# The second weight block decoded behind head 0's last exponential, and the decay sums written through GpSimd's queue: an attention and gated feed-forward kernel

## The chip, the cores and the metric

The program runs on one core of one Trainium2 chip. The time is device microseconds of one execution. The engines are TensorE (PE; its weight loads are PEld), VectorE (DVE), ScalarE (ACT), GpSimd (POOL) and SyncE (SP). SP does nothing but issue transfers; ACT and POOL issue some too, and such an instruction stands in the engine's own order like any other.

## The reference

```python
# q, k, v: (8, 8, 576, 64) f32; s: (8, 8, 576) f32; w_gate, w_val: (512, 1536); w_out: (1536, 512)
scores = scale * np.matmul(q, k.transpose(0, 1, 3, 2))
s_pos = np.maximum(s, 0.0)
cum = np.cumsum(s_pos, axis=-1)
bias = -(cum[:, :, :, None] - cum[:, :, None, :])
scores = np.where(causal, -1000000000.0, scores + np.minimum(bias, 0.0))
scores = scores - np.max(scores, axis=-1, keepdims=True)
attn = np.exp(scores)
attn = attn / (np.sum(attn, axis=-1, keepdims=True) + 1e-09)
x = np.matmul(attn, v)            # heads side by side: (4608, 512)
gate = 1.0 / (1.0 + np.exp(-(x @ w_gate)))
return (gate * (x @ w_val) @ w_out)
```

The three weights arrive as 64-bit floats (8 bytes for each number), so the kernel reads them as pairs of 32-bit words and builds 32-bit floats from them itself.

## The kernel before

**Attention.** 64 heads (8 batches of 8) are taken one after the other. A head has five query tiles, t = 4 down to 0, of 128 rows (the last of 64) against 576, 448, 320, 192 and 64 keys. A loop over ticks n emits one tile in each: scores on TensorE (`n_s`, L631, with a matmul that adds the mask, L518), one tick later the masked maximum on VectorE (`n_max`, L643) and the exponential on ScalarE (L644), then transposes of the exponentials (`n_turn`, L653, copied by ScalarE, L654) and the product with v (`n_av`, L662). Heads 0 to 7 are in f32; for these q and k are transposed on TensorE (`n_prep`, L614) and moved by ScalarE (L618, L619, L621). Later heads use f16 high and low parts and DMA transposes.

**Decay sums.** `cum` and `rel` hold the sums of all 64 heads, one head in a partition. `rel` is written to `cum_d` in DRAM (L167). Head 0's row is spread to 128 partitions by GpSimd from `rel` (L451); the row of each later head is read back from `cum_d` into `cr` (L447, SP's queue) and then spread (L451). `cr` has two buffers. `rel` shares the buffers tagged `rl` with the first loads of v for its squares (L184, GpSimd's queue).

**Weights.** Twelve blocks of w_gate and w_val (f = 0 to 11, 128 columns of each, 512 KB each in two transfers) and six of w_out are decoded in steps n. `weight_step` first issues the loads for which room comes free (`load_weight`; L284 on SP for blocks 0 and 1, L286 and L279 on ScalarE's queue for the rest), except in step 0, and then decodes its own block: a scaled copy on ScalarE (L298), three bit operations on VectorE (L299, L300, L301), eight small matmuls for the columns' bound (L310), their maximum (L313), the power of two of the scale (L332, L334), and the split into f16 high (ScalarE, L337) and low part (VectorE, L338). Raw words lie in `ws` for f divisible by 3, and else in parts of `w2all`, which is free until w_out's blocks are split into it; `t2f` and `io` are also used as room. Step 1 issues the loads of blocks 2 and 3.

**Feed-forward.** From tick 44 on, groups of 256 tokens by 128 hidden columns are put between the heads: 48 matmuls into `gv` (L714), tanh (L719), products (L721, L729, L730) and the output product (L745).

**Order.** A scheduler sets the order on each engine from the order of the code, priorities (`first()` raises that of heads 0 to 7) and its own simulated times; `tc.issue_after(ins)` makes it place what is inside behind `ins`. What runs on the chip is that fixed order on each engine, with semaphores between the engines. Before, steps 0 and 1 are both emitted at tick 0.

## Time and profile before

| | |
|---|---|
| runs | 1146.3, 1140.69, 1143.78 us; median 1143.78 |
| profiled execution | 1143.07 us |
| its span, first to last instruction | 1141.3 us |
| busy: PE, DVE, ACT, POOL | 1091.1, 829.2, 753.0, 201.2 us |
| granted TensorE clock, mean | 0.99 |

The page counts busy time of each engine over the span, and it names lines of the kernel (L298 is line 298). A group or row "out<-in" gives the buffers without their numbers; "[1.69 <-PE nt_ps L653]" behind a row is the idle time before it and what ended that. A row "SPq" or "ACTq" is an engine's issue of a transfer. In the table of stretches, PEclk is the granted clock and "DMA share" the mean busy share of the 16 DMA engines.

### The profile page before, as it was taken

To read this page: it belongs to the slowest core of one execution; us is meant where nothing else is said; L and a number is where in the kernel's file an instruction comes from. 1 tells how busy PE (TensorE), PEld (TensorE's weight loads), DVE (VectorE), ACT (ScalarE), POOL (GpSimd) and SP (SyncE) were. 2 spreads that over 40 slices of the span, in tenths; PEclk is the share of its full clock that TensorE was granted. 3 is DMA by queue.
4 is the path that set the end of the run, shared out by engine and by line. 5 is a ranking of instruction groups with operands and counts; after the bars stand their busy time and mean duration, and the time that the engine had idled before them with its cause. 6 is when DMAs were issued, how large, how long until landed. Compare 5 with 4: busy or idle time off the path is not lost.

```text
span 1141.3 us, 30312 instructions
## 1 busy us (share of the span) xinstructions
PE 1091.1 (96%) x11796; PEld 854.8 (75%) x11796; DVE 829.2 (73%) x2357; ACT 753.0 (66%) x1474; POOL 201.2 (18%) x471
## 2 busy tenths in 40 slices
PE   6897878899999999999999999999999999999998
PEld 4776766757787787788777777778877887787775
DVE  6758989876787777766565577777777779682854
ACT  5868667767786777676656577768776666343533
POOL 3302101022232222221111112212121212000000
PEclk9999889999999999999999999999999999999999
DMA  9776896997989798775736469787977664200000
GB/s 270 215 206 140 180 165 144 183 186 163 174 176 173 158 177 162 155 152 116 169 66 149 103 152 164 150 166 156 179 134 164 145 117 93 41 20 2 20 1 37
DMA packets 445357, 157.62 MB, mean 138 GB/s; under 512 B 403551, under 2 KB 435295, under 8 KB 445214
## 3 DMA queue, kind: packets, MB, share of 16 engines
q1 hardware_dynamic: 418974, 128.17, 57.6%
q10 hardware_dynamic: 23040, 16.78, 5.0%
q0 software_dynamic: 3200, 10.75, 2.6%
q8 instruction: 92, 1.51, 0.5%
q14 instruction: 51, 0.42, 0.1%
HBM read 56.92 MB, written 9.58 MB: 58 GB/s over the span
## 4 chain that ended last, share of the span: by engine, by line
PE 70%; DMA 9%; DVE 8%; issue 5%; ACT 4%; SPq 2%; POOL 1%; ACTq 0%; POOLq 0%; DVEq 0%
PE gv L714 33%; PE o L745 21%; PE tv L831 3%; PE s L491 3%; PE s L489 2%; DMA v<-in_v_dram 2%; PE ta L831 1%; DVE e L529 1%; PE av L564 1%; PE av L562 1%; PE av L563 1%; PE na_ps L662 1%; DMA T<-qk 1%; DMA w2all<-in_moe_w_out_dram 1%; DMA x<-x 1%
## 5 line engine op out<-in xcount | busy, mean ns | idle before, releaser
L714 PE MATMUL gv<-x,w 128*128 128x256 f16 (+3 forms) x6336 | 553.9, 245 | 9.8 <-DVE t2f L721 8.8
L714 PEld LDWEIGHTS <-w 128*128 128x128 f16 x6336 | 480.2, 98 | 63.4 <-issue 12.0
L745 PE MATMUL o<-w2all,h 128*128 128x512 f16 x1296 | 313.9, 379 | 1.9 <-ACT h L729 1.9
L530 ACT ACTIVATE e<-e,em 128x576 f32<-128x576 f32 x280 | 153.1, 556 | 88.8 <-DVE em L529 86.0
L745 PEld LDWEIGHTS <-h 128*128 128x128 f16 x1296 | 123.4, 98 | 109.1 <-ACT h L729 2.3
L511 POOL TENSOR_SCALAR_AFFINE_SELECT rl<-rl 128x128 f32<-128x128 f32 (+1 forms) x240 | 88.4, 369 | 499.2 <-DVE em L529 456.2
L529 DVE CUSTOM_DVE_ANT_0 e<-s,rl,qkcf 128x576 f32<-128x576 f32 x280 | 151.2, 544 | 28.8 <-PE s L491 12.8
L729 ACT ACTIVATE h<-t,hsc 128x256 f16<-128x256 f32 x192 | 96.3, 503 | 92.7 <-DVE t L721 90.4
L719 ACT ACTIVATE th<-gv,scb 128x256 f32<-128x256 f32 (+3 forms) x264 | 99.0, 403 | 65.5 <-PE gv L714 53.9
L539 DVE SCALAR_TENSOR_TENSOR p<-e,p 128x384 f16<-128x384 f32 x224 | 103.2, 499 | 41.1 <-ACT p L534 40.3
L721 DVE SCALAR_TENSOR_TENSOR t<-th,gv 128x256 f32<-128x256 f32 x168 | 69.7, 415 | 63.9 <-ACT th L719 63.8
L534 ACT ACTIVATE p<-e 128x1152 f16<-128x1152 f32 x112 | 111.9, 1000 | 3.4 <-DMA pt<-p 0.9
L730 DVE SCALAR_TENSOR_TENSOR h<-t,hsc,h 128x256 f16<-128x256 f32 x192 | 93.4, 487 | 27.4 <-ACT h L729 25.0
L562 PE MATMUL av<-v,pt 128*128 128x65 f16 x560 | 67.7, 193 | 2.5 <-DMA pt<-p 2.5
L451 POOL PARTITION_BROADCAST cr<-cr x63 | 59.4, 949 | 55.9 <-ACT th L719 21.1
L489 PE MATMUL s<-T 128*128 128x288 f16 (+2 forms) x246 | 64.5, 280 | 3.8 <-DVE em L529 3.0
L563 PE MATMUL av<-v,pt 128*128 128x64 f16 x560 | 67.7, 192 | 0.0
L564 PE MATMUL av<-v,pt 128*128 128x65 f16 x560 | 67.6, 194 | 0.0
L491 PE MATMUL s<-T 128*128 128x288 f16 (+2 forms) x246 | 61.5, 277 | 4.0 <-DMA T<-T 4.0
L562 PEld LDWEIGHTS <-pt 128*128 128x128 f16 x560 | 52.5, 98 | 8.3 <-DMA pt<-p 3.4
L563 PEld LDWEIGHTS <-pt 128*128 128x128 f16 x560 | 52.5, 97 | 4.5
L564 PEld LDWEIGHTS <-pt 128*128 128x128 f16 x560 | 52.7, 97 | 0.2
(209 smaller groups left out, 1539.9 us busy)
## 6 DMA issues: line engine op xcount, KB each, us to landing
v<-v SPq DMA_DIRECT2D x56, 162.5 KB
v<-in_v_dram SPq DMA_DIRECT2D x64, 128.0 KB
out_dram<-io POOLq DMA_DIRECT2D x32, 256.0 KB, 3.4
T<-T SPq DMA_DIRECT2D x82, 72.0 KB
t2f<-in_v_dram SPq DMA_DIRECT2D x20, 288.0 KB
qk<-in_q_dram SPq DMA_DIRECT2D x17, 288.0 KB
qk<-in_k_dram SPq DMA_DIRECT2D x17, 288.0 KB
w2all<-in_moe_w_gate_dram ACTq DMA_DIRECT2D x7, 512.0 KB
```

What stands on the lines that cost most here:

```text
L491: nc.tensor.matmul(ps[:, : b_ - a], lhs, T[i][:, 2, a:b_], start=False, stop=not mask)
L529: nc.vector.tensor_tensor_reduce(e, ps, r, c, MASKED, ALU.add, ALU.min, acc)
L530: nc.scalar.activation(e_t[t][:, :w], e_t[t][:, :w], AF.Exp, bias=acc, scale=-1.0)
L534: nc.scalar.activation(p_s[h_][:, 0], e_s[h_], AF.Copy, scale=PSCALE)
L539: nc.vector.scalar_tensor_tensor(flat[:, LOW[t] * P : (LOW[t] + t) * P], e_t[t][:, : t * P], PSCALE, flat[:, kb * P : (kb + t) * P], ALU.m ...
L562: nc.tensor.matmul(AV[i][:, t], hi, v_[:, D : 2 * D + 1], start=kb == 0, stop=False)
L563: nc.tensor.matmul(AV[i][:, t, 0:D], hi, v_[:, 0:D], start=False, stop=False)
L564: nc.tensor.matmul(AV[i][:, t], lo, v_[:, D : 2 * D + 1], start=False, stop=False)
L714: nc.tensor.matmul(ps[:, gv, a:e], w1[f][:, cc, gv, wl], x_of(b, cc)[:, xl, c0 + a : c0 + e], start=(c == 0), stop=(c == 3 * NC - 1))
L719: nc.scalar.activation(th[:, a:e], ps[:, 0, a:e], AF.Tanh, scale=scb[b][:, f : f + 1])
L729: nc.scalar.activation(h[:, 0], t2, AF.Copy, scale=hsc[:, f : f + 1])
L745: mm = nc.tensor.matmul(ps[:m], h[:, hl, tt * P : tt * P + m], w2[f][:, wl], start=(f == 0 and c == 0), stop=(f == NF - 1 and c == 2))
```

## The change

The write of `rel` to DRAM goes from SP's queue to GpSimd's. Step 1 is emitted at tick 5 instead of tick 0, and everything in it (its decode and the loads of blocks 2 and 3) is placed behind the exponential of head 0's tile 0, which is head 0's last. Steps 2 to 5 keep their ticks.

```diff
-    nc.sync.dma_start(cum_d, rel)
+    nc.gpsimd.dma_start(cum_d, rel)
...
-    qT, kT, nA = {}, {}, {}
+    qT, kT, nA, e_last = {}, {}, {}, []
...
-        nc.scalar.activation(e_t[t][:m, :w], e_t[t][:m, :w], AF.Exp, bias=acc, scale=-1.0)
+        ins = nc.scalar.activation(e_t[t][:m, :w], e_t[t][:m, :w], AF.Exp, bias=acc, scale=-1.0)
+        if (i, t) == (0, 0):
+            e_last.append(ins)
...
-            while n < NE and wnext["step"] < min(2 + n // 8, 6):
-                weight_step()
+            while n < NE and wnext["step"] < min((1 if n < NTL else 2) + n // 8, 6):
+                with tc.issue_after(e_last[0].ins) if wnext["step"] == 1 else ExitStack():
+                    weight_step()
```

Lines behind L644 carry numbers that are two or three higher in the changed kernel.

ScalarE at the start, from block 0's decode to head 0's last exponential. `e_80` holds tiles 4 and 3, `e_79` tiles 2, 1 and 0; "w2all<-w2all" is the decode of block 1. Before:

```order
L298 ACTIVATE wa_147<-ws_146 128x1024
L644 ACTIVATE e_80<-e_80,em_4_248 128x576
L298 ACTIVATE w2all<-w2all 128x1024
L644 ACTIVATE e_80<-e_80,em_3_274 128x448
L654 COPY p_1_82<-nt_ps_4_6_269 128x384
L186 ACTIVATE vsq_0_263,vss_262<-vsq_0_263 128x576
L286 DMA ws_146<-in_moe_w_gate_dram 128x4x256
L644 ACTIVATE e_79<-e_79,em_2_292 128x320
```

And now, from the same decode on:

```order
L644 ACTIVATE e_80<-e_80,em_3_249 128x448
L656 COPY p_1_82<-nt_ps_4_6_244 128x384
L656 COPY p_1_82<-nt_ps_3_3_257 128x384
L644 ACTIVATE e_79<-e_79,em_2_267 128x320
L656 COPY p_1_82<-nt_ps_3_0_262 128x384
L644 ACTIVATE e_79<-e_79,em_1_281 128x192
L644 ACTIVATE e_79<-e_79,em_0_301 64x64
L286 DMA w2all<-in_moe_w_gate_dram 128x4x256
L337 ACTIVATE w_0_66<-wa_147,wscale 128x8x128
L286 DMA w2all<-in_moe_w_val_dram 128x4x256
L186 ACTIVATE vsq_0_238,vss_237<-vsq_0_238 128x576
L286 DMA ws_146<-in_moe_w_gate_dram 128x4x256
```

Head 0's second exponential now follows its first, block 1's decode stands after the last row shown, behind head 0's fifth exponential, and the load of block 2 (into `w2all`) is ahead of that of block 3 (into `ws`). Block 2's decode stands behind head 1's second exponential.

SP's queue at the start, as a difference; `ws` and `w2all` are the loads of blocks 0 and 1, `v_0_159` is pair 0's v:

```order
 L284 DMA ws_146<-in_moe_w_val_dram 128x4x256
 L284 DMA w2all<-in_moe_w_gate_dram 128x4x256
-L167 DMA cum_d<-rel 64x576
 L284 DMA w2all<-in_moe_w_val_dram 128x4x256
 L463 DMA v_0_159<-in_v_dram 128x4x64 x2
 L464 DMA v_0_159<-in_v_dram 64x2x64
```

On GpSimd the issue stands directly ahead of the spreading of head 0's row (L451).

ScalarE later, where w_out's blocks are loaded and decoded, from the issue of a load into `t2f` (L279 and L286, just ahead of the first row) over a load into `w2all` to that block's decode ("wa_147<-w2all"). Before:

```order
L337 ACTIVATE w2all<-io,wscale 128x1024
L502 ACTIVATE rl_2784<-cr_2678,qkcf_2664 128x576
L502 ACTIVATE rl_2915<-cr_2795,qkcf_2664 128x576
L279 DMA w2all<-in_moe_w_out_dram 128x8x128
L286 DMA w2all<-in_moe_w_out_dram 128x8x128
L719 ACTIVATE th_9_1765<-gv_9_1740,scb_1272 128x256
L337 ACTIVATE w2all<-wa_147,wscale 128x1024
L428 ACTIVATE qk_13_2803<-qk_6_2262,qksc_2662 96x6x64
L430 ACTIVATE qk_13_2803<-qk_6_2262,qksc_2662 96x6x64
L298 ACTIVATE io<-ws_146 128x1024
L719 ACTIVATE th_10_1793<-gv_10_1768,scb_1272 128x256
L298 ACTIVATE wa_147<-w2all 128x1024
```

Now, between the two loads:

```order
L721 ACTIVATE th_5_1461<-gv_5_1436,scb_1272 128x256
L502 ACTIVATE rl_2784<-cr_2678,qkcf_2664 128x576
L337 ACTIVATE w_11_77<-w2all,wscale 128x8x128
L530 ACTIVATE e_80<-e_80,em_4_2698 128x576
L721 ACTIVATE th_6_1574<-gv_6_1549,scb_1272 128x256
L530 ACTIVATE e_80<-e_80,em_3_2754 128x448
L428 ACTIVATE qk_13_2803<-qk_6_2262,qksc_2662 96x6x64
L430 ACTIVATE qk_13_2803<-qk_6_2262,qksc_2662 96x6x64
L337 ACTIVATE w2all<-io,wscale 128x1024
L534 ACTIVATE p_1_82<-e_80 128x1152
L279 DMA w2all<-in_moe_w_out_dram 128x8x128
L286 DMA w2all<-in_moe_w_out_dram 128x8x128
```

And from there to the decode:

```order
L721 ACTIVATE th_7_1602<-gv_7_1577,scb_1272 128x256
L337 ACTIVATE w2all<-wa_147,wscale 128x1024
L530 ACTIVATE e_79<-e_79,em_2_2774 128x320
L530 ACTIVATE e_79<-e_79,em_1_2781 128x192
L530 ACTIVATE e_79<-e_79,em_0_2792 128x64
L473 ACTIVATE v_6_2797<-v_6_2758,vsc_967 128x10x64
L502 ACTIVATE rl_2915<-cr_2795,qkcf_2664 128x576
L298 ACTIVATE io<-ws_146 128x1024
L583 ACTIVATE x_4_2746<-xq_2260 128x640
L721 ACTIVATE th_8_1735<-gv_8_1710,scb_1272 128x256
L534 ACTIVATE p_0_81<-e_79 128x768
L298 ACTIVATE wa_147<-w2all 128x1024
```

There are ten instructions between the two loads instead of three, and eleven between the second load and its decode instead of six; the exponentials of one head (L530) and their copies (L534) have come in between. All queues are reordered in this way over the first third of VectorE's instructions; behind that the order on each engine is the one of before.

## The prediction

> **What bounds the kernel now.** The first part of the page says which engine fills the span; each row is busy time, share and count.

> ```profile
> span 1141.3 us, 30312 instructions
> PE 1091.1 (96%) x11796; PEld 854.8 (75%) x11796; DVE 829.2 (73%) x2357; ACT 753.0 (66%) x1474; POOL 201.2 (18%) x471
> ```

> TensorE is idle for 1141.3 - 1091.1 = 50.2 us in all. A table of stretches shows where.

> ```profile
> core 0: us, PE busy (x) PEld busy (x) DVE busy (x) ACT busy (x) POOL busy (x), PEclk, DMA share, GB/s
> 10.00:30.00 20.00, 15.16 (x107) 11.84 (x105) 14.04 (x39) 13.49 (x25) 4.48 (x7) 0.91 1.04 301
> 30.00:107.00 77.00, 68.80 (x530) 57.16 (x530) 53.97 (x156) 62.04 (x131) 16.02 (x26) 0.98 0.71 187
> 107.00:160.00 53.00, 41.64 (x456) 34.72 (x454) 53.00 (x150) 40.05 (x63) 4.00 (x7) 0.94 0.77 159
> 160.00:180.00 20.00, 17.32 (x167) 13.94 (x167) 14.52 (x31) 8.14 (x14) 1.90 (x4) 0.83 1.03 203
> ...
> 340.00:1100.00 760.00, 758.01 (x8560) 595.97 (x8558) 537.29 (x1527) 486.12 (x959) 134.86 (x328) 1.00 0.62 124
> ```

> From 340 us on TensorE has 2.0 us idle in 760, so that part has a fixed length, and what can change is when it begins. Ahead of it no engine is full but VectorE from 107 to 160 us (53.00 of 53.00); elsewhere engines wait for each other in turn. The chain of work that ended last shows the first such wait (start, length, what):

> ```profile
> 8.20 7.67 DMA w2all<-in_moe_w_val_dram
> ...
> 15.89 1.12 ACT w2all L298
> 17.01 0.56 ACT e L644
> ```

> The load of the second weight block (block 1) lies on the chain for 7.67 us, then its decode on ScalarE, then an exponential of head 0. Instructions, not a fixed date, follow on the chain, so time taken out here moves what comes behind it. ScalarE's own rows in that place (start, length, line, operation, wait before it):

> ```profile
> 15.89 1.12 ACT L298 ACTIVATE w2all<-w2all 128x1024 f32<-128x1024 f32 x1 [3.56 <-DMA w2all<-in_moe_w_val_dram]
> 16.91 0.66 ACT L644 ACTIVATE e<-e,em 128x448 f32<-128x448 f32 x1
> ...
> 17.82 0.70 ACT L186 ACTIVATE vsq<-vsq 128x576 f32<-128x576 f32 x1
> ...
> 20.03 0.35 ACT L644 ACTIVATE e<-e,em 64x64 f32<-64x64 f32 x1
> ...
> 23.11 0.48 ACT L654 COPY p<-nt_ps 128x384 f32<-128x384 f32 x1 [1.69 <-PE nt_ps L653]
> ...
> 24.22 0.40 ACT L618 ACTIVATE nq<-nq_ps 64x288 f32<-64x288 f32 x1 [0.62 <-DVE wscale L334]
> ...
> 25.07 1.15 ACT L337 ACTIVATE w<-w2all,wscale 128x1024 f16<-128x1024 f32 x1
> ...
> 28.12 1.33 ACT L644 ACTIVATE e<-e,em 128x576 f32<-128x576 f32 x2
> 29.36 1.13 ACT L298 ACTIVATE wa<-ws 128x1024 f32<-128x1024 f32 x1
> ...
> 33.92 1.15 ACT L298 ACTIVATE w2all<-w2all 128x1024 f32<-128x1024 f32 x1
> ```

> And VectorE's:

> ```profile
> 10.50 0.76 DVE L643 CUSTOM_DVE_ANT_0 e<-s,cr 128x576 f32<-128x576 f32 x1 [2.85 <-PE s L518]
> ...
> 14.11 0.08 DVE L643 DVE_READ_ACCUMULATOR2_ANT em<- 128x1 f32 x1
> ...
> 21.55 1.22 DVE L301 SCALAR_TENSOR_TENSOR w2all<-w2all 128x1024 int32<-128x1024 int32 x1
> ...
> 22.76 1.28 DVE L338 SCALAR_TENSOR_TENSOR w<-wa,wscale,w 128x1024 f16<-128x1024 f32 x1
> ...
> 24.79 0.76 DVE L643 CUSTOM_DVE_ANT_0 e<-s,cr 128x576 f32<-128x576 f32 x1 [0.69 <-POOL cr L451]
> ```

> The maximum of head 0's second tile is read out by 14.19 us, but its exponential starts at 16.91: ScalarE stands 3.56 us in the decode ahead of it.

> **Term 1: the decode of block 1 behind head 0's exponentials.** In the new order the second exponential can start at 14.2 instead of 16.91, 2.7 us earlier. From it to the last one (20.03) it took 3.1 us with a square of about 0.7 in between, which now comes later, so the last one keeps the 2.7 at least: 17.3.

> From there to head 1's first exponential it took 28.12 - 20.03 = 8.1 us. In this stretch the split of block 1 (1.15) goes out, to come two heads later, and its decode (1.12) and a square (0.7) come in: 8.8 us, so 26.1 if ScalarE's waits there (1.69 and 0.62) stay, and 23.8 if both go. VectorE's 24.79 + 0.76 = 25.6 is where the exponential's input is ready if nothing of head 1 moves there; 23.8 asks it to come earlier too. Head 1's first exponential so starts 2.0 to 4.3 us earlier, of which 1.15, the owed split, is paid back on ScalarE: 0.9 to 3.2. The owed VectorE work (a row like 21.55 and one like 22.76, 2.5 us) is covered by VectorE's idle 23.0 of 77 us from 30 to 107; with that cover gone it would cost the 2.5.

> The step also issues the loads of blocks 2 and 3 on ScalarE's queue. They pass no transfer on SP or GpSimd; block 3 was first of the two, and now block 2 is, with its second half behind block 0's split, so near 18.5. Block 2's decode stood at 33.92 and now stands behind head 1's second exponential, at 25.1 to 27.4, with head 1's third exponential queued behind it and the transposes on TensorE behind that. At the 7.67 us that block 1's half took, block 2's lands at 26.2: a new wait of 0 to 1.1 us. Term 1 is then between 0 (0.9 less 1.1) and -3.2. I take -2.5, nearer the far end, as the removed wait is read directly and the new one only bounded.

> **Term 2: the decay sums through GpSimd's queue.** SP's rows and the wait on it:

> ```profile
> 4.74 0.51 SPq L284 DMA_DIRECT2D w2all<-in_moe_w_gate_dram  x1
> 7.67 0.48 SPq L167 DMA_DIRECT2D cum_d<-rel  x1
> 8.20 0.59 SPq L284 DMA_DIRECT2D w2all<-in_moe_w_val_dram  x1
> ...
> 19.00 10.99 SPq L447 DMA_DIRECT2D cr<-cum_d  x3
> ```

> ```profile
> SPq L167 <- DVE rel L166: 2.3, 1, 2.3
> ```

> SP waited 2.3 us for `rel` and issued for 0.48; block 1's second half and everything behind it can be issued 2.9 us earlier. On GpSimd, and (last row) the time from issue to landing of the loads that it issued up to 60 us:

> ```profile
> 7.74 0.86 POOL L451 PARTITION_BROADCAST cr<-rel  x1
> ...
> 12.78 0.55 POOL L184 DMA_DIRECT2D vsq<-in_v_dram  x1 [3.61 <-DMA cum_d<-rel]
> ...
> 23.52 1.24 POOL L451 PARTITION_BROADCAST cr<-cr  x1 [4.07 <-DMA cr<-cum_d]
> ```

> ```profile
> DMA to landing us min/median/max: 3.2/5.5/6.9
> ```

> The issue costs GpSimd 0.55 us (as the row of 12.78; the longest of its kind 0.73), so head 0's broadcast ends at 9.2 to 9.3 instead of 8.6. Its reader starts at 10.50, after a wait for TensorE: 1.2 us of cover, cost 0; with the cover gone, 0.7. Issued from GpSimd, such transfers land in 3.2 to 6.9 us, so the sums are in DRAM by 15.3; head 1's row is read back at 19.00, or 16.1 when SP runs 2.9 ahead. The gain is 0 to 2.9 us for head 1's broadcast (23.52), already inside term 1's bounds, as ScalarE is not free before 23.8. I add 0. It need not all come: the DMA engines' share from 10 to 30 us is 1.04, so issuing earlier mostly reorders a full queue.

> [...]

> **Term 3: the order further on.** The scheduler reorders all queues, but only in the part that lies before some 300 us. The place that I can price is where weights of the output product are loaded on ScalarE's queue.

> ```profile
> 156.98 1.28 ACTq L286 DMA_DIRECT2D t2f<-in_moe_w_out_dram  x1
> ...
> 159.74 3.79 ACTq L286 DMA_DIRECT2D w2all<-in_moe_w_out_dram  x1
> ...
> 163.63 0.47 ACT L719 ACTIVATE th<-gv,scb 128x256 f32<-128x256 f32 x1 [2.85 <-issue]
> ...
> 171.08 1.14 ACT L298 ACTIVATE wa<-w2all 128x1024 f32<-128x1024 f32 x1 [2.82 <-DMA w2all<-in_moe_w_out_dram]
> ```

> ```profile
> 172.25 0.69 DVE L299 TENSOR_SCALAR w2all<-wa 128x1024 int32<-128x1024 int32 x1 [3.30 <-ACT wa L298]
> ```

> The issue at 159.74 takes 3.79 us and holds ScalarE for 2.85, and the decode that reads the load waits 2.82 more; VectorE, full before, idles 20 - 14.52 = 5.5 us here. The new order puts ten ScalarE instructions instead of three between the load of 156.98 and that of 159.74, and eleven instead of six between the latter and its decode; such instructions take 0.3 to 1.1 us each in the rows above, so the transfers get some 5 and 3 us more. Gain at most VectorE's 5.5; the other end is a loss of as much, for the same reshuffling could build such a place elsewhere. I take -2.0.

> **Sum.** -2.5 + 0 - 2.0 = -4.5 against the profiled execution, 1143.07 us (span 1141.3 and 1.8 around it): 1138.6. The median of three runs is 1143.78, 0.7 above it. About 0.5% (5.7 us) is what a measurement of this kernel can tell from no change, so the forecast counts as the same.

> **Rivals.** (a) Both gains come whole: -3.2 - 5.5 = -8.7, 1134.4, faster. For it: the waits removed at both places are in ScalarE's order, and the rows show nothing between them and TensorE's full stretch. Against: from 107 to 160 us VectorE is full, and work that reaches it earlier only queues there. (b) Nothing is left: the start is bound by transfers (share 1.04 from 10 to 30 us), block 2 lands late by what was gained, and term 3 is 0: about 1143. [...] (c) Slower: block 2's decode stands ahead of head 1's third exponential, and block 2 lands late. Before, that decode ran at 33.92, and the trace does not show by how much it had landed sooner; landing only then would hold ScalarE 33.9 - 25.1 = 8.8 us, against a gain of 2.5: 1143.1 + 6.3 = 1149.4. It decides from a landing near 27.6 us, where wait and gain are equal. Against it: block 3, then the first of the two, was decoded at 29.36 without a wait, behind loads that began at the same time. (d) The decode does not move out of the way: excluded by the new order, where it stands behind the fifth exponential.

> **Chances.** Forecast (-1.5 to -5.7) 0.38; (a) 0.33; (b) 0.15; (c) and other losses in the new order 0.14. So faster 0.33, same 0.53, slower 0.14. Range: down to 1131, a little below (a) since term 3 is bounded by one place only; up to 1148, inside (c), leaving a tenth on each side. The forecast's own range is 1137.5 to 1141.5.

> **What would show it.** In the new profile the exponential of head 0's second tile starts near 14.2 and the last one by 17.3; head 1's first at 23.8 to 26.1; SP issues block 1's second half near 5.3 and `cum_d` stands on GpSimd near 7.7, with the broadcast over by 9.3; the wait of 3.56 us on ScalarE is gone; ScalarE's two waits near 160 to 171 are under 2 us together. From 340 us on nothing differs but the start. The forecast is wrong if ScalarE waits over 2.5 us for block 2 near 26 us, if head 1 waits for its decay row as long as before, or if VectorE idles elsewhere between 107 and 250 us.

## The result, and the profile after

The changed kernel is slower by 0.54%: median 1150.13 us of 20 executions (1144.98 to 1156.67) against 1144.23 us of 20, ratio 1.0054 with a 95% interval of 1.0040 to 1.0068, or +6.2 us. (One of the 20 of before took 5687.02 us and is left out of the ratio; the median of the other 19 is 1144.02.) The forecast was 1138.6, its range ended at 1148. The traced execution, 1145.96 us (span 1144.2), is one of the shortest of the 20; a second traced one took 1147.69. The first two lines of its page, and the stretches of the prediction's table:

```profile
span 1144.2 us, 30324 instructions
...
PE 1090.7 (95%) x11796; PEld 856.0 (75%) x11796; DVE 831.9 (73%) x2357; ACT 755.5 (66%) x1474; POOL 210.5 (18%) x472
```

```profile
core 0: us, PE busy (x) PEld busy (x) DVE busy (x) ACT busy (x) POOL busy (x), PEclk, DMA share, GB/s
10.00:30.00 20.00, 16.72 (x132) 13.26 (x131) 15.59 (x41) 16.05 (x32) 4.92 (x8) 1.00 1.06 305
30.00:107.00 77.00, 66.89 (x509) 55.39 (x508) 55.94 (x160) 60.70 (x123) 15.68 (x25) 0.96 0.70 187
107.00:160.00 53.00, 37.90 (x411) 31.68 (x410) 52.26 (x143) 37.98 (x61) 9.18 (x8) 0.87 0.79 170
160.00:180.00 20.00, 17.36 (x202) 14.84 (x199) 18.74 (x51) 15.37 (x28) 2.53 (x5) 0.91 1.06 215
340.00:1100.00 760.00, 757.98 (x8563) 596.27 (x8561) 539.84 (x1535) 490.18 (x964) 138.77 (x332) 1.00 0.61 125
```

Up to 30 us TensorE does more than before (16.72 us busy and 132 records, against 15.16 and 107). From 30 to 160 us it does less, 104.8 against 110.4, and its granted clock from 107 to 160 is 0.87 against 0.94. From 340 us on nothing differs. ScalarE at the start, answering the rows of before:

```profile
13.74 0.67 ACT L644 ACTIVATE e<-e,em 128x448 f32<-128x448 f32 x1 [1.68 <-DVE em L643]
...
16.25 0.69 ACT L644 ACTIVATE e<-e,em 128x192 f32<-128x192 f32 x2
17.35 0.44 ACTq L286 DMA_DIRECT2D w2all<-in_moe_w_gate_dram  x1
...
20.07 1.14 ACT L298 ACTIVATE w2all<-w2all 128x1024 f32<-128x1024 f32 x1 [0.41 <-DMA nqk<-in_k_dram]
...
24.77 1.34 ACT L644 ACTIVATE e<-e,em 128x576 f32<-128x576 f32 x2
26.01 1.15 ACT L298 ACTIVATE w2all<-w2all 128x1024 f32<-128x1024 f32 x1
```

Head 0's second exponential starts at 13.74 (before 16.91), its last two end at 16.94, head 1's first starts at 24.77 (28.12), and block 2's decode at 26.01 waits for nothing. SyncE and GpSimd:

```profile
5.30 0.51 SPq L284 DMA_DIRECT2D w2all<-in_moe_w_val_dram  x1
```

```profile
7.96 0.72 POOL L167 DMA_DIRECT2D cum_d<-rel  x1 [0.26 <-DVE rel L166]
8.72 0.86 POOL L451 PARTITION_BROADCAST cr<-rel  x1
```

And ScalarE where term 3 was priced, now without the waits of 2.85 and 2.82 us:

```profile
156.11 0.68 ACTq L286 DMA_DIRECT2D w2all<-in_moe_w_out_dram  x1
...
162.36 1.11 ACT L298 ACTIVATE io<-ws 128x1024 f32<-128x1024 f32 x1
165.07 1.15 ACT L298 ACTIVATE wa<-w2all 128x1024 f32<-128x1024 f32 x1
```

So the places that the prediction looked at went as it said, or nearly, and the time did not. How the lead ran out can be read from the starts of single exponentials (us; the first tanh is that of the first feed-forward unit):

| | head 1 | head 3 | head 4 | head 6 | head 8 | first tanh |
|---|---|---|---|---|---|---|
| before | 28.12 | 47.19 | 62.32 | 83.76 | 100.80 | 120.96 |
| changed | 24.77 | 40.77 | 61.67 | 82.85 | 100.65 | 129.65 |
| difference | -3.4 | -6.4 | -0.7 | -0.9 | -0.2 | +8.7 |

A second trace of before has heads 4, 6 and 8 at 61.49, 82.89 and 99.70 and the first tanh at 119.91, so differences of up to 1.1 us say nothing here. The lead of 6.4 us is gone between heads 3 and 4, and between head 8 and the first feed-forward unit nearly 9 us are lost. The stretches in question, first before, then the changed kernel:

```profile
40.00:50.00 10.00, 9.76 (x74) 8.04 (x72) 8.53 (x28) 8.25 (x19) 2.69 (x7) 1.00 0.91 271
...
73.00:77.00 4.00, 3.51 (x39) 3.18 (x37) 1.94 (x10) 3.30 (x10) 0.85 (x1) 1.00 0.53 150
...
105.00:126.00 21.00, 13.96 (x145) 11.06 (x143) 21.00 (x62) 18.32 (x30) 1.69 (x3) 0.92 0.72 157
```

```profile
40.00:50.00 10.00, 7.12 (x58) 6.32 (x57) 9.16 (x16) 9.94 (x21) 4.33 (x5) 0.89 0.45 131
50.00:60.00 10.00, 9.96 (x65) 8.57 (x64) 6.59 (x17) 6.54 (x14) 2.01 (x4) 0.77 0.92 257
...
73.00:77.00 4.00, 2.31 (x16) 1.39 (x16) 3.88 (x6) 3.93 (x12) 0.86 (x1) 1.00 0.80 232
77.00:90.00 13.00, 11.09 (x74) 8.68 (x74) 5.62 (x21) 7.39 (x18) 1.37 (x3) 1.00 0.60 160
...
105.00:126.00 21.00, 10.20 (x77) 7.30 (x75) 21.00 (x58) 16.89 (x28) 4.16 (x4) 0.68 0.79 178
```

The fourth busy figure is ScalarE's: 9.94 of 10 from 40 to 50 us and 3.93 of 4 from 73 to 77, and TensorE, the first figure, drops to 7.12 and 2.31. Behind the first of these its clock falls (0.89, 0.77). From 105 to 126 VectorE is full in both kernels, but in the changed one TensorE gets 10.20 us of work and a clock of 0.68. What makes ScalarE full at 40 to 50 us:

```profile
38.68 2.19 ACT L337 ACTIVATE w<-w2all,wscale 128x1024 f16<-128x1024 f32 x2
...
43.81 1.16 ACT L298 ACTIVATE w2all<-w2all 128x1024 f32<-128x1024 f32 x1
...
46.39 1.13 ACT L298 ACTIVATE w2all<-w2all 128x1024 f32<-128x1024 f32 x1
47.40 0.57 ACT L644 ACTIVATE e<-e,em 128x320 f32<-128x320 f32 x1
```

The owed split of block 1 stands with block 2's ahead of head 3 (2.19 us), and the decodes of blocks 4 and 5 stand between head 3's second and third exponentials; before, only block 5's stood there.

### The profile page after: what moved, and what is told of

It reads as the page before. It is cut to its first block, busy times and chain, and to the rows that moved or that the text cites. A ratio compares the mean times of both kernels' runs of the same rounds, so it can differ in the third digit from the quotient of the medians.

```text
span 1144.2 us, 30324 instructions
## 1 busy us (share of the span) xinstructions
PE 1090.7 (95%) x11796; PEld 856.0 (75%) x11796; DVE 831.9 (73%) x2357; ACT 755.5 (66%) x1474; POOL 210.5 (18%) x472
## 3 DMA queue, kind: packets, MB, share of 16 engines
HBM read 56.92 MB, written 9.58 MB: 58 GB/s over the span
## 4 chain that ended last, share of the span: by engine, by line
PE 71%; DVE 9%; DMA 7%; issue 6%; ACT 4%; POOL 2%; SPq 2%; ACTq 0%; POOLq 0%; DVEq 0%
PE gv L716 33%; PE o L747 21%; PE tv L833 3%; PE s L491 3%; PE s L489 2%; PE ta L833 1%; DVE e L529 1%; DMA v<-in_v_dram 1%; PE av L564 1%; PE av L562 1%; PE av L563 1%; DMA T<-T 1%; DVE p L539 1%; POOL rl L511 1%; POOL cr L451 1%
## 5 line engine op out<-in xcount | busy, mean ns | idle before, releaser
L530 ACT ACTIVATE e<-e,em 128x576 f32<-128x576 f32 x280 | 154.0, 557 | 92.1 <-DVE em L529 88.2
L534 ACT ACTIVATE p<-e 128x1152 f16<-128x1152 f32 x112 | 112.0, 1000 | 4.0 <-DMA pt<-p 1.4
L732 DVE SCALAR_TENSOR_TENSOR h<-t,hsc,h 128x256 f16<-128x256 f32 x192 | 93.5, 488 | 27.4 <-ACT h L731 25.0
L451 POOL PARTITION_BROADCAST cr<-cr x63 | 63.9, 1020 | 53.8 <-DMA cr<-cum_d 38.9
L491 PE MATMUL s<-T 128*128 128x288 f16 (+3 forms) x246 | 62.2, 280 | 9.8 <-DMA T<-T 9.8
L489 PE MATMUL s<-T 128*128 128x288 f16 (+3 forms) x246 | 63.9, 278 | 7.0 <-DVE em L529 3.8
L562 PE MATMUL av<-v,pt 128*128 128x65 f16 x560 | 69.0, 194 | 1.2 <-DVE xq L577 0.9
L564 PE MATMUL av<-v,pt 128*128 128x65 f16 x560 | 68.8, 195 | 0.0
```

The source lines that it names most:

```text
L491: nc.tensor.matmul(ps[:, : b_ - a], lhs, T[i][:, 2, a:b_], start=False, stop=not mask)
L530: nc.scalar.activation(e_t[t][:, :w], e_t[t][:, :w], AF.Exp, bias=acc, scale=-1.0)
L534: nc.scalar.activation(p_s[h_][:, 0], e_s[h_], AF.Copy, scale=PSCALE)
L562: nc.tensor.matmul(AV[i][:, t], hi, v_[:, D : 2 * D + 1], start=kb == 0, stop=False)
L564: nc.tensor.matmul(AV[i][:, t], lo, v_[:, D : 2 * D + 1], start=False, stop=False)
```

## The experiments

Each ratio below is against executions of before that were taken along with that run (their medians lie between 1143.77 and 1145.86 us).

**Each part alone, scheduler free.** The first kernel is before with only the queue changed (`nc.gpsimd.dma_start(cum_d, rel)`), the second the changed kernel with that line back on `nc.sync`.

> The kernel before with the decay sums alone on GpSimd's queue; the weight step stays where it was. Theory A (the changed kernel loses its lead by the order in which the scheduler then puts the work on ScalarE and VectorE: decodes of blocks 4 and 5 ahead of head 3's exponentials, and the split of pair 3's x late at 122-127 us, so that TensorE starves at 105-126 us): this kernel has neither of these fully, so it should be within 3 us of before, 1141 to 1147, with head 0's exponentials as before (last one near 20 us). Rival B (it is the transfer through GpSimd's queue that costs: it lands later, or holds up GpSimd's issues): all of the loss is here already, 1148 to 1152. Rival C (any new order of the work scatters the time by some us, with no one place to blame): anywhere from 1140 to 1150.

> The changed kernel with the decay sums back on SyncE's queue: the move of the weight step alone. Here the scheduler leaves the decode of block 4 behind head 4's exponentials (as before) and puts the split of pair 3's x 9 to 17 rows earlier on VectorE than in the changed kernel. Theory A: the early lead (first exponential of head 1 at 24 to 26 us) is kept longer and the first feed-forward unit starts by 124 us: 1140 to 1146. Rival B: the GpSimd part gone, 1142 or less whatever the order. Rival C: 1140 to 1150.

Measured: 1152.38 us, ratio 1.0073 (1.0046 to 1.0100), and 1155.33, 1.0101 (1.0074 to 1.0129). The step alone lost more than both parts together, the queue alone at least as much (its interval covers the 1.0054 of both). Theories A and C allowed neither of the two: both lie above C's 1150 as well. B's figures nearly fit the first kernel and not the second. What both have in common with the changed kernel is that the scheduler put out another order.

**Two mends of the order, scheduler free.**

```diff
# first: the decode of blocks 8 and later behind the split of pair 3's x
+    with tc.issue_after(x_last[-1].ins) if wnext["step"] >= 8 else ExitStack():
         weight_step()
# second: steps 4 and 5 behind head 3's last exponential (e_last[1])
-    with tc.issue_after(e_last[0].ins) if wnext["step"] == 1 else ExitStack():
+    with tc.issue_after(e_last[0 if wnext["step"] == 1 else 1].ins) if wnext["step"] in (1, 4, 5) else ExitStack():
```

> The changed kernel, with the decode of weight blocks 8 and later put behind the last split of pair 3's x. Its order up to row 205 of ScalarE and VectorE is that of the changed kernel; then pair 3's x split is 15 rows earlier on VectorE and the first feed-forward unit 8 rows earlier on ScalarE. Theory A: the lead in heads 3 and 4 is still given back (lag about 0 at 100 us), but TensorE no longer starves at 105 to 126 us: first tanh of the feed-forward units by 123 us (129.65 in the changed kernel, 120.96 before), under 5 us of halved clock there instead of 13.65, and 1143 to 1146.5. Rivals B: 1148 to 1152, as the start is unchanged. Rival C: 1140 to 1152 without a tie to the feed-forward's start.

> The changed kernel, with the decode of blocks 4 and 5 put behind head 3's last exponential, as it stood before. From head 5 on the scheduler's order is then nearly that of the kernel before. Theory A: the lead of head 3 (6 us) survives the stretch at 40 to 60 us by half or more, nothing starves at 105 to 126 us (first tanh of the feed-forward by 121 us), and the time is 1138 to 1142.5, the prediction's. Rival B: 1148 to 1152, as the GpSimd part is in it. Rival C: 1140 to 1150. If the order is before's from head 5 on and the early lead is still there at 60 us but not at the end, then the lead is given back further on whatever the order, 1142.5 to 1145.

(In the second text "as it stood before" holds for neither block: before, block 4's decode stood ahead of head 2's exponentials and block 5's between head 3's second and third.) Measured: 1152.05, 1.0076 (1.0056 to 1.0097): no gain, although in its trace the first tanh came 19.1 us behind head 8 instead of 29.0; so the late x split is not by itself the loss. And 1145.35, 1.0017 (0.9996 to 1.0038): most of the loss gone, with the GpSimd part in it, so B falls. In its one traced execution (1141.39 us) head 4 starts at 57.84, head 8 at 96.67 and the first tanh at 116.69, 4 us ahead of before throughout; at the end of that execution 1.7 us are left of it (1141.39 against 1143.07), and over twelve executions none of it shows.

**The order held.** From here on each engine's order is written out and forced by edges between neighbours, so that a part can be changed without a new order coming with it. In outline:

```diff
+    for name in written_order[engine]:
+        if last is not None:
+            tc.add_manual_dep(traced[name], last, NoSync)
+        last = name
```

> The kernel before with each engine's instructions held in before's order by written edges, and only the decay sums' transfer taken off SyncE's queue and put on GpSimd's, directly ahead of head 0's spreading. With the scheduler free, this same edit cost 8 us. Theory B (the transfer through GpSimd's queue costs): 1149 to 1153 again. Theory C (the scheduler's new order costs): 1142 to 1145, as before; by term 2 of the prediction, 0 to -3 against before.

> The changed kernel's order on every engine, held by written edges, with only the decay sums' transfer put back on SyncE's queue at its old place. Theory B: the loss goes, 1141 to 1145. Theory C: the order carries the loss, 1147 to 1152, with a mean granted clock near 0.982 as in the changed kernel.

Measured: 1144.03, 1.0006 (0.9991 to 1.0022), and 1149.91, 1.0054 (1.0033 to 1.0075). The queue costs nothing in before's order, and putting it back gains nothing in the new one. The same edit that cost 8 us with the scheduler free cost nothing with the order held. The order carries the loss.

**Which half of it.** The two orders joined at the first scores of head 8.

> The changed kernel with its own order on every engine up to the first scores of head 8, and before's order from there on, all held by written edges. Theory F (the loss sits in the new order of heads 0 to 7: ScalarE full with the owed split and the decodes near 40-50 and 73-77 us, TensorE under about half busy there, and its clock then halved): 1147 to 1152. Theory G (it sits behind that: VectorE's new order ahead of the split of pair 3's x, TensorE starved at 109-123 us): 1142 to 1146.

> The reverse: before's order on every engine up to the first scores of head 8 (with the decay sums on GpSimd's queue), and the changed kernel's order from there on. Theory F: 1142 to 1146. Theory G: 1147 to 1152. If both halves carry a part, both of these kernels lie at 1146 to 1149.

Measured: new order first 1151.02, 1.0051 (1.0031 to 1.0071); old order first 1146.24, 1.0018 (1.0002 to 1.0034). Heads 0 to 7 carry nearly all, the order behind them some 2 us, though the trace of the changed kernel shows its largest gap (105 to 126 us) in that later part. Work that VectorE, full there in both orders, does early it need not do later: from 160 to 180 us TensorE has 202 records in the changed kernel and 167 before.

**The same kernels traced again.**

> The kernel before once more, for a second traced execution of the same instructions. If the halved stretches of the clock follow from where an execution falls against a grid of 3.41 us, they are in part at other places than in the first trace (16.9, 34.0, 115.9, 126.2, 160.3 us), those behind the long waits at 111 and 158 us come again, and the time is 1140 to 1148. The exponential of head 0's second tile starts at 16.9 again, whatever the clock.

> The changed kernel once more. Its first traced execution was one of the fastest of 20 (1145.96 us, clock 0.986); the middle one had 1150 us and 0.982. If the missing 4 to 5 us are halved clock in the stretch at 73-90 us, where three other kernels with the same order had 13.7 us of it and the first trace had none, they show here: with a halved stretch there 1149 to 1156 us and a lag of 4 to 6 us at 80 us, without one 1144 to 1148 us.

Measured: 1144.06 us with the clock at half from 18.8, 114.3, 124.6, 162.1 and 298.6 us, so four of the five places of the first trace came again, 1.6 to 1.9 us away, and 34.0 did not; head 0's second exponential at 17.12. And 1147.69, without a halved stretch at 73 to 90 us, as the text expected of such an execution. Six traces have the new order in heads 0 to 7 (one of them with the added matmuls described next). In the three without that stretch (changed kernel twice, new order then old) the times are 1145.96, 1147.69 and 1145.65; in the three with 13.7 us of it (the kernel with the x split first, that with the new order and SyncE's queue, and the filled one) 1155.70, 1153.28 and 1153.77. The kernel with the new order and SyncE's queue:

```profile
73.00:77.00 4.00, 2.35 (x16) 1.82 (x17) 2.81 (x5) 3.96 (x10) 1.26 (x1) 0.93 0.62 175
77.00:90.00 13.00, 12.83 (x52) 10.98 (x52) 2.70 (x7) 4.82 (x12) 0.03 (x1) 0.50 0.58 159
```

At 73 to 77 us this is the changed kernel's row again, 2.35 against 2.31 of 4.00 with ScalarE full. Behind it the clock is 0.50 where it was 1.00, TensorE is busy for 12.83 of 13 us and gets 52 matmuls done instead of 74. Head 6 starts at 87.49 instead of 82.85.

**Filling TensorE's waits.** Added matmuls at places where TensorE waited, in the held orders.

> The changed kernel's order held on every engine, plus 112 matmuls that TensorE runs where it stood waiting for over 1.4 us (ahead of head 2's product with v, of the first feed-forward unit, and within the scores of heads 10, 12, 14, 16 and 20): they write what is overwritten, or add zeros, and take some 0.13 us each at full clock. Theory D (the new order's waits on TensorE let its clock be halved, and it is the halved clock, 20 us of lost clock over a run against 11 before, that makes the run longer): fewer halved stretches, mean clock up from 0.982 to 0.986 or more, time 1143 to 1147. If the clock is only a companion of the waits: the same as the changed kernel or some us more, 1150 to 1156.

> The kernel before in its own order, held, plus 96 such matmuls at its own waits (scores of heads 8, 14 and 20, and ahead of feed-forward units 2, 8 and 10). Theory D: the halved stretches at 126, 160 and 164 us go; clock above 0.991; 1139 to 1143. If the clock is only a companion of the waits: 1143 to 1149.

Measured: 1153.71, 1.0071 (1.0046 to 1.0096), mean clock 0.9863; and 1145.75, 1.0015 (1.0002 to 1.0027), clock 0.9914. The clock rose as theory D said (from 0.9823 and 0.9903) and the time did not fall: both lie outside D's ranges and inside those for a clock that is only a companion of the waits. The added matmuls did not all fit into waits, though: in the second one's trace TensorE is busy for 11.0 us more than before (1102.1 against 1091.1) and idle for only 7.4 less. As a remedy it is out; whether the clock alone would have given the time back it does not tell.

**One place in heads 0 to 7.** Between head 5's second and third exponentials the changed kernel has three ScalarE instructions for weights, here in ScalarE's rows:

```profile
68.85 1.15 ACT L337 ACTIVATE w<-w2all,wscale 128x1024 f16<-128x1024 f32 x1
70.52 1.16 ACT L298 ACTIVATE io<-t2f 128x1024 f32<-128x1024 f32 x1 [0.52 <-DMA t2f<-in_moe_w_out_dram]
...
71.95 1.14 ACT L298 ACTIVATE w2all<-w2all 128x1024 f32<-128x1024 f32 x1
...
72.98 0.56 ACT L644 ACTIVATE e<-e,em 128x320 f32<-128x320 f32 x1
```

The first three kernels move them (and in two of them head 3's) behind the head's last exponential.

> The changed kernel with its own order held on every engine, but for four instructions: on ScalarE the split of block 4 and two decodes (1.1 us each), which stood between head 5's second and third exponentials, go behind head 5's last one, and VectorE's part of that split goes behind head 5's last maximum. Theory H (one place carries most of it: these 3.4 us make ScalarE full at 73-77 us, TensorE is busy 2.3 of 4.0 us there, and in half of the executions its clock is then halved for 13.7 us): TensorE at 3.4 or more of 4.0 us there, no halved stretch at 76-90 us, 1144 to 1147. Theory I (the loss is spread over the order of heads 0 to 7): 1148 to 1152.

> As the kernel before it, and the decodes of blocks 4 and 5, which stood between head 3's second and third exponentials on ScalarE, go behind head 3's last one. Theory H with term 1: the lead of 6 us at 50 us is then kept in part, no halved stretch near 48-55 us, 1140 to 1145. Theory I: 1147 to 1151.

> The same two moves, with before's order on every engine from the first scores of head 8 on (as in the run with the new order first and the old one behind it, 1151.0). Theory H with term 1, and the 2 us of the later order saved as well: 1138.5 to 1143. Theory I: 1146 to 1151.

Measured: 1153.66 (1.0072; 1.0057 to 1.0087), 1157.80 (1.0115; 1.0091 to 1.0139) and 1155.20 (1.0084; 1.0065 to 1.0103). All miss the ranges of both theories, because the edit made the place worse: pair 3's copies of q (L619) then stood behind the moved work, and TensorE behind those, as its row in the first of them shows:

```profile
76.88 0.47 PE L614 MATMUL nq_ps<-ident,nqk 96*128 96x96 f32 x3 [3.92 <-ACT nq L619]
```

One wait of 3.92 us, and head 6 starts at 88.30 with the clock at half from 77.8 to 91.4 us. The next two kernels move the three instructions, with what waits for them, into ScalarE's gap behind those copies, which shows in the changed kernel as the wait ahead of head 6:

```profile
82.85 0.78 ACT L644 ACTIVATE e<-e,em 128x576 f32<-128x576 f32 x1 [4.55 <-DVE em L643]
```

> The changed kernel's order held, and the same three ScalarE instructions (3.4 us, between head 5's second and third exponentials) moved further than in the first try, behind pair 3's copies of k, where the traces show ScalarE waiting 4.55 us and VectorE 4.85 us for head 6; the transfers that wait for them and VectorE's part go with them. In the first try they stood ahead of pair 3's copies of q, and TensorE waited 3.92 us for these. Theory H: TensorE busy 3.3 or more of 4.0 us at 72-76 us, no halved stretch at 76-90 us, 1144 to 1147. Theory I (spread loss): 1148 to 1152, whatever happens at that place.

> The same move, and before's order on every engine from the first scores of head 8 on. Theory H, with the 2 us of the later order saved: 1141 to 1145. Theory I: 1147 to 1151.

Measured: 1149.05, 1.0036 (1.0021 to 1.0050), and 1146.85, 1.0012 (0.9994 to 1.0031). Their rows for 73 to 77 and 77 to 90 us, one kernel after the other:

```profile
73.00:77.00 4.00, 2.73 (x20) 1.93 (x19) 0.70 (x3) 3.93 (x11) 0.86 (x1) 1.00 0.03 7
77.00:90.00 13.00, 10.76 (x63) 8.77 (x62) 8.43 (x22) 8.37 (x16) 1.26 (x3) 0.87 0.83 229
```

```profile
73.00:77.00 4.00, 3.39 (x29) 2.61 (x27) 0.85 (x3) 3.93 (x12) 0.86 (x1) 1.00 0.03 9
77.00:90.00 13.00, 10.02 (x63) 7.80 (x64) 8.04 (x21) 8.38 (x16) 0.61 (x2) 1.00 0.84 231
```

With the old order behind, seven moved ScalarE instructions and transfers and four of VectorE's took the time from 1.0051 to 1.0012, 4.4 us of the 5.8. With the new order behind they took it from 1.0054 to 1.0036, 2.1 us, which their intervals do not tell from nothing, and TensorE reached 2.73 of 4.00 us there, not the 3.3 expected. By the ranges, 1149.05 is theory I's, and 1146.85 lies between the two, next to I's. So one place in heads 0 to 7 is shown to carry the greater part only when the later order is the old one; with the new order behind, a spread loss is not excluded. No kernel beat before: the nearest are the held order with the GpSimd queue (1.0006) and this one.

The main kernels with the granted clock (mean over the executions; "lost" is span times one minus clock, at most what halving took):

| order of heads 0-7 / later | ratio | clock | lost, us |
|---|---|---|---|
| old / old (before) | 1 | 0.9903 | 11.1 |
| old / old, GpSimd queue | 1.0006 | 0.9895 | 12.0 |
| old / new | 1.0018 | 0.9861 | 15.9 |
| new, head 5 mended / old | 1.0012 | 0.9878 | 13.9 |
| new / old | 1.0051 | 0.9853 | 16.9 |
| new, head 5 mended / new | 1.0036 | 0.9853 | 16.9 |
| new / new, SyncE queue | 1.0054 | 0.9833 | 19.1 |
| new / new (changed) | 1.0054 | 0.9823 | 20.3 |

The changed kernel loses up to 9.2 us more to the halved clock than before, which is more than its whole loss. Of the kernels not in the table, those without added matmuls run from 12.5 us lost at 1.0017 (blocks 4 and 5 later) to 25.1 at 1.0115. Within the changed kernel's 20 executions time and clock go together (correlation -0.86): 1144.98 us at 0.990, 1156.67 at 0.975. But the clock alone does not order the kernels: old / new lost 15.9 us at 1.0018, new / old 16.9 at 1.0051. And TensorE need not be busy throughout a halved stretch: in the changed kernel's first trace it was busy for 5.43 of the 13.65 us that were halved from 112.6 us on.

## Why the prediction was wrong

**What failed in term 1.** The step that failed is "instructions, not a fixed date, follow on the chain, so time taken out here moves what comes behind it", with only the owed split of 1.15 us paid back, and the owed VectorE work covered "by VectorE's idle 23.0 of 77 us". The cover was taken from the mean over 77 us, and only of VectorE. On ScalarE, 62.04 of those 77 us were busy, and the new order piled the weight work into 40 to 50 us (9.94 of 10) and 73 to 77 us (3.93 of 4). The payback was 5.8 us between heads 3 and 4, not 1.15. Even so the 0.7 us left at head 4 lie inside the term's range of 0 to 3.2: in this trace term 1 accounts for a gain that did not come, not for the loss. The start itself was sized well: exponentials at 13.74 (14.2 predicted), the last two over by 16.94 (the last to start by 17.3), head 1 at 24.77 (23.8 to 26.1).

**What failed in term 3.** This is the step that turned the sign: the new order was taken at -2.0 us from one place. That place went right: both waits gone, VectorE 18.74 of 20 us busy instead of 14.52. Its two ends, plus and minus 5.5 us, stood for an order that changes everywhere up to 300 us. "The other end is a loss of as much" was given as a bound, from no row of the places where a loss could be built. The runs put the loss far ahead of the place that was priced: the new order of heads 0 to 7 alone costs 1.0051, or 5.8 us. This should have been the widest term; the runs show orders from 1.0006 to 1.0115 for nearly the same instructions.

**A missing term.** Every duration was taken at the clock of the one trace. The prediction's own table had the clock at 0.94 and 0.83 in the stretches in question, and no term asked what a reshuffled order would do to it: it was put at nothing, without a reason. Its mean fell from 0.9903 to 0.9823, up to 9.2 us.

**Term 2** was right in its sum: 1.0006 (0.9991 to 1.0022) with the order held, against 0. Its working was not: in that kernel head 1's first exponential starts at 26.38 instead of 28.12, so SyncE's earlier issue does move the start by up to 1.7 us (its trace also lacks the halved stretch that before has at 16.9 us), and the time does not show it. GpSimd's broadcast ended at 9.58, 0.3 later than worked out, ahead of its reader (VectorE's row of 10.49). The issue took 0.72 us.

**Rivals.** (c) had the sign but not the mechanism: block 2 did not come late. What came is what its chance of 0.14 also stood for, "other losses in the new order". (a) and (b) fell. None of the three named signs of a wrong forecast was the one that came: ScalarE did not wait for block 2, the decay row came in time, and VectorE was not idle but busy with other work (131.17 of the 143 us from 107 to 250, against 129.60 before).

**Open.** The kernel with blocks 4 and 5 later has 4 us of lead in its trace up to the first tanh and no gain over twelve executions (0.9996 to 1.0038). One trace does not tell what the other eleven did with it; they run from 1141.13 to 1152.57 us, again with the clock (correlation -0.85). Nor is it shown by a kernel how much of the loss is the clock and how much the waits that bring it on: none changed the one without the other. The traces allow an estimate, from TensorE's busy time and its idle time (span less busy), in us:

| traced execution | time | TensorE busy | TensorE idle |
|---|---|---|---|
| before | 1143.07 | 1091.1 | 50.2 |
| before, second trace | 1144.06 | 1091.5 | 50.8 |
| changed | 1145.96 | 1090.7 | 53.5 |
| changed, second trace | 1147.69 | 1091.1 | 54.8 |
| new / new, SyncE queue | 1153.28 | 1098.0 | 53.5 |
| new / old | 1145.65 | 1095.5 | 48.4 |

In the three traces of the whole new order the waits add some 3 to 5 us each time, and the longer busy time under a halved clock adds from nothing to 7 us, depending on the execution. With the old order behind head 8, TensorE waits no longer than before, and the whole difference in that trace is busy time, some 4 us.

## What to carry to other kernels

Where a scheduler sets the order, an edit is two changes: what it says, and a new order for everything behind it. Price the second as a spread, from what reordered variants of the kernel do, or hold the order by written edges and measure the edit by itself; here that turned +8 us into +0.7, which its interval does not tell from zero. Look for cover on the engine and in the few microseconds where the owed work will stand, not in an average over the stretch, and before moving work behind something, look at what waits behind that.

## What the runs showed of the hardware

```profile
73.00:76.40 3.40, 1.75 (x13) 1.32 (x14) 2.21 (x3) 3.36 (x9) 1.26 (x1) 1.00 0.61 177
76.40:79.80 3.40, 3.23 (x16) 2.86 (x17) 1.80 (x4) 3.10 (x8) 0.00 (x0) 0.50 0.64 158
79.80:83.20 3.40, 3.40 (x15) 3.11 (x15) 0.00 (x0) 0.11 (x1) 0.00 (x0) 0.50 0.97 318
```

And the changed kernel at the same place, in steps laid by its own halved stretches (one begins at 47.7 us):

```profile
71.62:75.03 3.41, 2.15 (x18) 1.56 (x16) 2.43 (x9) 3.40 (x9) 0.86 (x1) 1.00 0.57 168
75.03:78.45 3.42, 2.58 (x16) 1.77 (x17) 2.17 (x4) 3.21 (x9) 0.00 (x0) 1.00 0.77 216
```

TensorE busy for 1.75 of 3.40 us was followed by four halved steps; 2.15 of 3.41, at the same place of the same order, by none. The other four of the six traces agree: 1.88 and 1.89 of 3.41 us in the two with the halved stretch, 2.17 and 2.22 in the two without. It is no sharp limit. Counted over all 19 traces up to 400 us, in steps laid in this way, a step at full clock with TensorE busy for under 40% of it was followed by a halved one in all 70 cases, one of 40 to 60% in 27 of 90, and one of over 67% in none; in the first traces of before and of the changed kernel alone these are 8 of 8, 2 of 11 and 0 of 186.

Against the program the halved stretches move from execution to execution (47.7 us in one trace of the changed kernel, 49.5 in the other). A step with TensorE busy for half its time was enough in some cases (1.75 of 3.40 us above), and a halved stretch went on for four steps although TensorE was busy for 12.83 of 13 us in it; why it lasted so long no run shows. An order that leaves TensorE half idle for 3 us was therefore a gamble in this kernel, of 4.6 us at head 6 (87.49 against 82.85), taken anew in each execution: three of the six traces have that halved stretch.
